# Linear attention and an MLP in one kernel: another hand-set order of the same operations, with the first group's loads ahead of the second slice of w_in

## The chip, the cores and the metric

The kernel runs on one core of a Trainium2 chip. The metric is the device time of one execution in microseconds; each kernel's time is the median of several executions.

A core has five engines that run side by side, each through its own queue in order: PE (matrix products), DVE (vector work), ACT (activation functions, also copies), POOL (vector work, and here the issuing of all loads that convert from 32-bit to 16-bit floats), and SP (the issuing of the stores, of the transposes done by the DMA engines, and of one small load). An instruction waits for the data or the buffer that it needs, and everything behind it on its engine waits with it.

## The reference: what is computed

A causal attention with a decay per head, in blocks of 64 positions with a running state, and behind it an MLP with an exact GELU on all 3072 tokens (4 batches of 768):

```python
for b in range(nb):                       # 12 blocks of 64 positions
    intra = einsum('bhic,bhjc->bhij', qb, kb) * Dmask       # Dmask = lam ** (i - j), lower triangle
    intra = einsum('bhij,bhjd->bhid', intra, vb)
    inter = einsum('bhid,bhde->bhie', qb * lam_pow, kv_state)
    out[:, :, sl] = intra + inter
    kv_state = lam_block * kv_state + einsum('bhsd,bhse->bhde', kb * rev_pow, vb)
x = out.transpose(0, 2, 1, 3).reshape(3072, 512)
h = x @ w_in                              # 512 -> 2048
g = 0.5 * h * (1 + erf(h / sqrt(2)))
return g @ w_out                          # 2048 -> 512
```

## The kernel before

**Tiling.** The sequence is cut into six groups of 128 positions (g = 0 to 5). A group has 4 batches, taken as two pairs (p = 0, 1), so 512 tokens. Per group the kernel does the attention of both pairs, then the first product (x by w_in) with the GELU, and then the second product (by w_out) with the stores. Weights stay in SBUF. Accumulators are eight PSUM banks: M0, M1, M2 for the first product, N0, N1 mostly for transposes and the second product, X0, X1 for attention scores and outputs, KV for the state.

**The order is written out.** Each step is registered with a name, an engine, what it reads and what it writes. `emit` then issues the steps in the sequence of the text ORDER, so that ORDER sets the queue of each engine; the tile framework adds the waits that reads and writes need. Steps with a choice of engine (`"ACT|DVE"` and the like) go to the first one unless the name in ORDER has a suffix such as `/DVE`. The prices given with the steps serve a planner outside the kernel and have no effect when it runs.

**Names.** Digits are group and pair, then a part.

- `ld.q00a`, `ld.k00b`, `ld.v01a`: loads of q, k, v for group 0; a and b are the two batches of a pair (128 KB each, L323). `ld.q10` and so on: loads of a whole pair for later groups (256 KB, L316). `ld.wi0`, `ld.wi4`, `ld.wi8`, `ld.wi12`: four slices of w_in (512 KB, L336). `ld.wo00` to `ld.wo11`: four quarters of w_out (512 KB, L341). All are issued by POOL.
- `trow`, `tpos`, `tdl`, `tex`, `tmk`, `tid`, `cols`: small tables on DVE and PE (L200 to L239); `ln`, `etab`, `xv2`, `xg0`, `xg1`, `xx`, `xq`, `xv`, `xc`: powers of lambda on ACT (decay L243, lam_x L234); `tg0`, `tg1`: their masks on DVE; `gtab` (L279) loads the GELU table on ACT after the last of these.
- `idle0`, `idle1`, ...: dummy matmuls of 128x512 on zeros (L879), as many as IDLES says; `bits` is one more.
- `Tq00a`, `Tk00a`: transposes of q and k on PE for groups 0 and 1 (L550, L405); `Eq000`, `Ek000`: their copies out of PSUM (L304 on ACT, L306 on DVE). From group 2 the transposes are DMAs issued by SP (L416).
- Group 0: `sc000`, `sc001` scores; `m0000` and so on masks times decay (L611, DVE); `vh000` v scaled by the decay (L528); `o000`, `o001` outputs; `x000`, `x001` copies into x; `ka00a`, `ka00b` states and `sa00a` their decay. Later groups: `u` scores and first half of the state, `m`, `sm` (a copy of the state), `i` the contribution of the state and the second half, `o`, `x` (L517), `ks` and `sa`; `vh` scaled v (L366 ACT, L369 DVE or POOL).
- `H0.3.0`: first product of group 0, two columns of 128 (number 3 of 8) for pair 0, 8 matmuls of 128x256; `g0.3.0` its GELU (L673). `H0.0.x` and `H0.1.x` read ld.wi0, `H0.2.x` and `H0.3.x` ld.wi4, 4 and 5 ld.wi8, 6 and 7 ld.wi12. `h1.1.5`: one of seven products that replace eight (Strassen-Winograd) in later parts, with sums `V`, `X`, `W`, `S` and `hm`, `hs`, `ha`, `hb`, `g` around them. `Q0.0a` to `Q3.0d`: second product of group 0; `Q0.0b` reads ld.wo10. `P` with `pm`, `ps`, `pa`, `c11`, `c12`, `c21`, `c22`: second product of later groups; `st`, `sp`: stores.

**Buffers around the change.** Raw q, k and v have four buffers each, used in turn by group and pair; scaled v (`vh`) has two, so that `vh21` must wait until `o11` has read `vh11`. The sequence of the steps in which they are registered (L946 on) decides which of two steps on the same buffer comes first.

All matrix products are recorded with line L283, all copies with L304 or L306.

Of the kernel before, what the change touches and what calls it, by code (L numbers as in the profile page):

```python
# [30 lines left out]
sa11 V0.2 H0.4.1 g0.6.0 g0.6.1 H0.7.1 vh201/ACT o11 Tk21 H1.0.0 x111 vh211/POOL g0.4.1 g0.7.1 x110 H0.7.0 g1.0.0 X0.1
ld.wo00 Tq20 V2.1 h1.1.5 V0.0 H1.5.0 X1.1 hm1.1 X2.1 ks20 hs1.1/DVE H1.1.0 V0.3 Tk20 h1.1.6 g1.1.0 h1.1.2 g0.7.0
H1.0.1 g1.1.00 g1.5.0 H1.4.0 ha1.1 g1.0.1 Tq21 X3.1 H1.4.1 g1.4.0 V1.2 V3.2 h1.1.7 vh200 g1.4.1 H1.1.1 hb1.1 ld.v40
h1.3.5 V2.3 g1.1.1 W0.0 h1.1.3 ld.wo10 h1.1.4 V1.0 u20 g1.1.10 ld.wo01 H1.5.1 g1.1.01 m201 ld.wo11 sm20 m200 Q0.0a
g1.5.1 ld.v30 i20 ld.k30 h1.3.1 sa20 Q1.0a hs1.3 V1.3 ld.q30 V3.3 hm1.3 h1.3.6 g1.1.11 o20 ha1.3 ks21 ld.k31 h1.3.2
x201 vh210/ACT h1.3.3 x200 Q0.0b ld.v31 V3.0 u21 S0.1.2 S2.1.0 h1.3.7 sm21 V2.0 m211 Q1.0b g1.3.00 m210 Q0.0c hb1.3
Q1.0c S0.1.4 i21 Q0.0d sa21 S1.1.2 h1.3.4 W1.0 q0.0 Q1.0d ks30 g1.3.10 Q2.0a q1.0/DVE S0.1.0 o21 h2.0.1 x210 Q2.0b
hs2.0 x211 g1.3.01 Q3.0a X0.2 Tq30 g1.3.11 S3.1.2 X1.2 h2.0.5 S1.1.4 h2.0.6 X2.2 hm2.0 Tk30 vh300 Q2.0c ha2.0 Q3.0b
S0.1.6 h2.0.2 h2.0.7 Tk31 g2.0.00 vh311/POOL h2.0.3 hb2.0 h2.1.1 g2.0.01 X3.2 Q3.0c vh301/POOL vh310 h2.0.4 h2.1.5
g2.0.10 ld.q31 u30 hm2.1/DVE hs2.1 Q3.0d m300 sm30 ld.q40 m301 h2.1.6 q3.0 h2.1.2 ha2.1 g2.0.11 i30 g2.1.00 W0.1  # L40
h2.1.7 sa30/ACT S2.1.4 h2.1.3 hb2.1 h2.2.1 S0.2.0 g2.1.01 Q2.0d V2.2 ks31 Tq31 h2.1.4 g2.1.11 q2.0/DVE h2.2.5 g2.1.10
S2.1.2 o30 W1.1 hm2.2 sp0.1 P5.1a vh400/POOL sp0.0 hs2.2/DVE Tq40 P5.1b x301 vh401/POOL x300 h2.2.6 h2.2.2 ha2.2
ld.k40 u31 g2.2.00 sp0.2 h2.2.7 m310 sm31 P1.1a pm.1 ld.v41 hb2.2 m311 h2.3.1 h2.2.4 S1.1.0 S3.1.4 i31 g2.2.10 h2.2.3
hs2.3/DVE P1.1b g2.2.01 sa31 S0.2.2 h2.3.6 ps.1/DVE h2.3.5 S1.1.6 h2.3.2 Tk40 hm2.3 S2.1.6 o31 ks40 S3.1.0 P2.1a ha2.3
g2.2.11 sp0.3 x310 g2.3.00 h2.3.7 vh410/POOL h2.3.3 hb2.3 P2.1b S2.2.0 ld.v51 g2.3.11 x311 h2.3.4 c11.1 h3.0.1 W2.0
# [4 lines left out]
ld.q51 h3.2.1 S1.2.6 h3.1.4 S2.2.4 sm41/DVE P5.2a g3.1.10 c12.1/DVE g3.1.11 h3.2.5 m410 hs3.2 P5.2b hm3.2 S1.2.2 m411  # L50
h3.2.6 P1.2a S2.3.2 S3.2.4 S3.2.2 h3.2.2 ha3.2 i41 S3.2.0 Tq50 S0.3.0 h3.2.7 sa41 h3.2.3 hb3.2 P1.2b Tk50 g3.2.01
S1.3.0 g3.2.00 S3.2.6 h3.2.4 pm.2 S2.2.6 h3.3.5 ps.2 h3.3.1 o41 g3.2.10 st1.00 P2.2a vh510/POOL vh511 hs3.3 st1.11
ks50 st1.01 x411 h3.3.6 g3.2.11 P6.2a S2.2.2 hm3.3 x410 h3.3.2 ha3.3 P2.2b h3.3.7 h3.3.3 hb3.3 u50 g3.3.01 S0.3.4
# [72 lines left out]
def kernel(  # L126
# [207 lines left out]
    def add_w_in(kf0, kf1):  # L334
        f = slice(kf0 * 128, kf1 * 128)
        add("ld.wi%d" % kf0, "POOL", lambda: nc.gpsimd.dma_start(w_in[:, :, f], w_in_r[:, :, f]), (),  # L336
            ["wi%d.%d" % (kf, kh) for kf in range(kf0, kf1) for kh in range(2)], ("w", kf1 - kf0))
# [667 lines left out]
```

## Time and profile before

| | before |
|---|---|
| median of 3 runs | 207.84 us (206.88 to 209.09) |
| profiled execution, its own time | 207.61 us |
| its span, first to last instruction | 205.8 us |
| PE busy | 194.6 us (95%) |
| DVE busy | 145.6 us (71%) |
| ACT busy | 104.8 us (51%) |
| POOL busy | 62.2 us (30%) |
| dummy matmuls, without `bits` | 32 |

The profile is of one execution. Times are from the first instruction of the span. A row of records in order of time gives the start, the duration from the first start to the last end of the merged instructions, engine, line, operation, what it writes and reads, sizes and how many; in brackets stands how long the engine had been idle just before, and what ended that. Rows of groups give busy time in all and the mean of one in ns. Durations of matmuls contain the way through the array, so that the next may start before one ends; 16 matmuls of 128x256 end to end take about 1.75 us at full clock. "PEclk" is the clock that PE was granted, as a share of full speed. For loads the profile gives the time from the issue on POOL to the landing; KB are those of the 16-bit destination.

### The profile page before, as it was taken

To read this page: it belongs to the slowest core of one execution; us is meant where nothing else is said; L and a number is where in the kernel's file an instruction comes from. 1 tells how busy PE (TensorE), PEld (TensorE's weight loads), DVE (VectorE), ACT (ScalarE), POOL (GpSimd) and SP (SyncE) were. 2 spreads that over 40 slices of the span, in tenths; PEclk is the share of its full clock that TensorE was granted. 3 is DMA by queue.
4 is the path that set the end of the run, shared out by engine and by line. 5 is a ranking of instruction groups with operands and counts; after the bars stand their busy time and mean duration, and the time that the engine had idled before them with its cause. 6 is when DMAs were issued, how large, how long until landed. Compare 5 with 4: busy or idle time off the path is not lost. (4 is left out here: it accounts for less than half of the span.)

```text
span 205.8 us, 6791 instructions
## 1 busy us (share of the span) xinstructions
PE 194.6 (95%) x2955; PEld 155.4 (76%) x2955; DVE 145.6 (71%) x317; ACT 104.8 (51%) x211; POOL 62.2 (30%) x73
## 2 busy tenths in 40 slices
...
PEclk9999699999999999999999999999999999999999
...
GB/s 61 179 172 188 180 164 177 157 146 153 113 180 189 157 179 85 209 136 178 69 138 103 123 113 230 5 178 80 54 0 105 0 5 0 22 185 1 155 51 154
DMA packets 95598, 24.56 MB, mean 119 GB/s; under 512 B 85840, under 2 KB 95056, under 8 KB 95568
## 3 DMA queue, kind: packets, MB, share of 16 engines
...
q14 instruction: 7, 0.06, 0.1%
...
## 5 line engine op out<-in xcount | busy, mean ns | idle before, releaser
L765 ACT ACTIVATE g<-M 128x512 bf16<-128x512 f32 x51 | 29.9, 598 | 47.8 <-PE M L283 47.1
L283 PEld LDWEIGHTS <-w_in 128*128 128x128 bf16 x480 | 46.1, 99 | 9.0 <-issue 0.8
L283 PE MATMUL M<-x,w_in 128*128 128x256 bf16 x328 | 45.2, 279 | 1.3 <-DMA w_in<-in_moe_w_in_dram 0.7
L283 PEld LDWEIGHTS <-g 128*128 128x128 bf16 x304 | 29.2, 98 | 10.2 <-issue 2.1
L283 PE MATMUL N<-w_out,g 128*128 128x256 bf16 (+1 forms) x224 | 35.9, 303 | 0.8 <-DMA w_out<-in_moe_w_out_dram 0.8
L283 PEld LDWEIGHTS <-S 128*128 128x128 bf16 x320 | 30.9, 98 | 3.7
L369 POOL TENSOR_TENSOR vh<-vr,lam_v 128x256 bf16<-128x256 bf16 x18 | 12.0, 688 | 53.4 <-DMA vr<-in_v_dram 27.8
L283 PEld LDWEIGHTS <-V 128*128 128x128 bf16 x216 | 20.9, 98 | 4.2 <-issue 0.9
L283 PE MATMUL M<-xs,w_in 128*128 128x256 bf16 x136 | 20.5, 273 | 0.0
L283 PE MATMUL M<-xs,V 128*128 128x256 bf16 x136 | 19.4, 273 | 0.0
L673 ACT ACTIVATE g<-M 128x512 bf16<-128x512 f32 x24 | 13.3, 601 | 10.2 <-PE M L283 9.9
L283 PE MATMUL N<-T,S 128*128 128x256 bf16 x144 | 18.2, 273 | 0.0
L691 DVE TENSOR_TENSOR S<-g 128x512 bf16<-128x512 bf16 x40 | 16.4, 417 | 2.0 <-ACT g L765 2.0
L784 DVE TENSOR_TENSOR m<-m,M 128x512 f32<-128x512 f32 x17 | 11.7, 686 | 8.6 <-PE M L283 5.4
L283 PE MATMUL N<-w_out,S 128*128 128x256 bf16 x144 | 17.5, 273 | 0.0
L517 DVE TENSOR_TENSOR x<-X,lam_x 128x512 bf16<-128x512 f32 x20 | 13.2, 683 | 5.1 <-PE X L283 5.0
L283 PE MATMUL KV<-vh,kr 64*64 64x64 bf16 x352 | 15.9, 196 | 0.6 <-DVE vh L528 0.4
L485 DVE TENSOR_TENSOR scm<-X,mask 128x512 bf16<-128x512 f32 x20 | 13.3, 686 | 3.8 <-PE KV L283 3.8
L283 PEld LDWEIGHTS <-kr 64*64 64x64 bf16 x352 | 13.9, 108 | 1.1 <-issue 1.0
L316 POOL DMA_DIRECT2D vr<-in_v_dram x10 | 11.8, 1176 | 8.8 <-ACT g L673 7.1
L779 DVE TENSOR_TENSOR M<-m,M 128x512 f32<-128x512 f32 x17 | 11.7, 690 | 2.8 <-ACT g L765 1.7
L765 ACT ACTIVATE g<-m 128x512 bf16<-128x512 f32 x18 | 11.4, 634 | 1.6 <-DVE m L784 1.6
...
## 6 DMA issues: line engine op xcount, KB each, us to landing
out_dram<-osb SPq DMA_DIRECT2D x22, 256.0 KB, 2.5
vr<-in_v_dram POOLq DMA_DIRECT2D x10, 256.0 KB, 9.2
kr<-in_k_dram POOLq DMA_DIRECT2D x10, 256.0 KB, 9.5
qr<-in_q_dram POOLq DMA_DIRECT2D x10, 256.0 KB, 8.3
w_in<-in_moe_w_in_dram POOLq DMA_DIRECT2D x4, 512.0 KB, 8.0
w_out<-in_moe_w_out_dram POOLq DMA_DIRECT2D x4, 512.0 KB, 8.5
qr<-in_q_dram POOLq DMA_DIRECT2D x4, 128.0 KB, 5.7
kr<-in_k_dram POOLq DMA_DIRECT2D x4, 128.0 KB, 5.8
```

What stands on the lines that cost most here:

```text
L283: nc.tensor.matmul(*a, skip_group_check=True, **kw)
L316: add("ld.%s%d%d%s" % (n, g, p, suffix(cs)), "POOL", lambda: nc.gpsimd.dma_start(dst, source(n, g, p, cs)), (), rkeys(n, g, p, cs), ("load ...
L369: ENG[e].tensor_mul(o_[:, c, h0:h1], v_[:, c, h0:h1], lam_v[:, h0:h1, None].to_broadcast((128, h1 - h0, D)))
L485: add(name("m", hi), "DVE", lambda hi=hi: nc.vector.tensor_mul(m_[:, hi, cr], sc[hi][:, cr], mask[:, None, None, :].to_broadcast((128, nc_ ...
L517: add(name("x", bl), "DVE", lambda bl=bl: nc.vector.tensor_mul(x_[:, cr, :, half(bl)], o[bl][:, cr], lam_x[:, None, :, half(bl)].to_broadc ...
L673: lambda: nc.scalar.activation(gt[g % 2][:, 2 * j:2 * j + 2, t], seen(bk, "n t", n=2), ACT.Gelu),
L691: lambda i=i, op=op, l=l, r=r: nc.vector.tensor_tensor(s(i)[0], l[0], r[0], op), l[1] + r[1], s(i)[1],
L765: lambda: nc.scalar.activation(gt[g % 2][:, 4 * c + fo:4 * c + 3 + fo:2, th * 2 * C:(th + 1) * 2 * C], src, ACT.Gelu),
L779: add("ha" + nm, "DVE", lambda: nc.vector.tensor_add(seen(bc, "q t", q=2), f5, seen(bb, "q t", q=2)), [bb, k5], [bc], ("ps", 512))
L784: add("hb" + nm, "DVE", lambda: nc.vector.tensor_add(f7, f5, seen(bb, "q t", q=2)), [bb, k5], [k7], ("ps", 512))
```

## The change

ORDER is another sequence of the same operations, from its first line to the first product of group 3; behind that the two are alike. There are six groups of dummy matmuls instead of eight (26 matmuls instead of 32). For 31 steps the engine is another: 16 copies, products and scalings leave DVE (11 for ACT, 5 for POOL), 12 come to DVE from ACT, one goes from ACT to POOL, and two from POOL to ACT.

The loads of group 0 (twelve) now all stand ahead of ld.wi0, and ld.v10, which stood among them, stands behind ld.wi0, ld.q10, ld.k10 and three scalings that POOL does (vh000, vh011, vh010; before, POOL did vh000 and vh101 there). The tables xx and xq stand ahead of the first copies on ACT. ld.wo10, ld.wo01 and ld.wo11 stand right behind ld.wo00; before, ld.v40 stood between.

The three other edits do not change what is issued: the condition on neg2 and lam_q2 was false before too (PAIRED holds no 1), WSPLIT gives the slices that the loop gave, and 600 is a price for the planner.

```diff
-IDLES = (4, 13, 1, 1, 1, 3, 8, 1)
+WSPLIT = ((0, 4), (4, 4), (8, 4), (12, 4))
+IDLES = (3, 12, 1, 8, 1, 1)
 
 ORDER = """
-tb0 ldlam trow ld.wi4 ld.q00b ld.k00a idle0 tpos ln bits tdl etab ld.q00a tmk ld.k00b tid tex ld.v00a cols xv2 ld.v00b
-xg1 ld.k01b xg0 ld.q01b tg1 idle1 Tq00b ld.k01a Eq001/DVE idle2 Tk00a ld.q01a tg0 Ek000 idle3 Tq00a ld.v10 xv
-Eq000/DVE idle4 Tk00b Ek001 ld.v01b xc idle5 sc000 ld.v01a sc001 m0000 vh000/POOL m0001 m0010 vh001 ld.wi0 idle6 Tk01a
-o000 m0011 ld.k10 ka00a sa00a idle7 o001 ka00b x000 ld.q10 Tk01b x001 Ek011/DVE Tq01a Ek010/DVE xq xx Tq01b sa00b
-vh101/POOL H0.3.0 Eq011/DVE Eq010 vh010 ld.wi8 gtab sc011 vh011 sc010 ld.q11 V0.1 ka01a m0100 ld.k11 m0111 H0.1.0
-m0101 ld.v11 H0.0.0 sa01a m0110 o010 ld.wi12 g0.0.0 o011 Tk10 g0.1.0 ld.v21 x011 ka01b Ek101/DVE x010 vh100 Tq10
-ld.k20 sa01b H0.0.1 Eq100 Eq101/DVE Ek100 ks10/DVE H0.1.1 ld.v20 g0.0.1 g0.3.0 u10 ld.k21 H0.4.0 m100 m101 H0.2.1
+tb0 ldlam trow bits ld.wi4 ld.k00b ld.q00a idle0 tpos ln tdl etab ld.q00b tex ld.k00a cols tmk xv2 ld.q01b xg0 tid
+ld.v00a ld.v00b xg1 tg0 ld.q01a V0.1 xx ld.v01b tg1 idle1 Tq00a ld.k01b xq xv xc Eq000 Tq00b ld.v01a Tk00b Eq001/DVE
+Ek001 Tk00a ld.k01a Ek000/DVE gtab ld.wi0 idle2 sc000 sc001 m0000 ld.q10 m0011 m0001 ld.k10 m0010 idle3 o000 vh001
+vh000/POOL idle4 o001 x001 Tk01b x000 idle5 Tq01b vh011/POOL ka00a Ek011 Eq011/DVE Tq01a sa00a Tk01a Eq010 Ek010/DVE
+ka00b vh010/POOL H0.3.0 sa00b sc010 ld.v10 sc011 m0101 ka01a H0.0.0 m0111 ld.q11 m0100 H0.1.0 g0.0.0 m0110 ld.wi8 o010
+sa01a o011 ld.k11 Tq10 x010 ka01b g0.1.0 sa01b Tk10 x011 Ek101/DVE H0.0.1 ks10/DVE Ek100/DVE H0.1.1 vh100/ACT
+vh101/POOL Eq100/DVE Eq101/DVE V1.1 g0.1.1 ld.v11 u10 Tq11 m101 sm10 ld.wi12 H0.2.0 g0.0.1 m100 ld.k21 H0.2.1 g0.2.0
...
-        if 1 in PAIRED:
+        if 1 in PAIRED and 1 in QSG:
...
-                over(["x%d%d%d" % (g % 2, p, i) for i in range(2)], (ch,)), ("acp", 512))
+                over(["x%d%d%d" % (g % 2, p, i) for i in range(2)], (ch,)), ("acp", 600))
...
-    for s in range(0, NKF, 4):
-        add_w_in(s, s + 4)
+    for s, n in WSPLIT:
+        add_w_in(s, s + n)
```

The rest of group 0 and the loads behind it, as far as the prediction speaks of them (new order):

```
i10 ld.v20 g0.2.1 H0.3.1 sa10 ld.q21 Eq110/DVE H0.5.0 g0.3.1 g0.3.0 ld.k20 Tk11 Eq111 H0.4.0 g0.5.0 vh110/POOL vh111
o10 g0.4.0 H0.4.1 x100 Ek110 ks11 ld.q20 x101 H0.5.1 Ek111 ld.v21 u11 g0.5.1 V0.3 h1.1.1 m110 sm11 H0.6.1 g0.4.1 m111
...
V1.0 H1.5.1 V2.3 g1.1.1 X2.1 Tk21 V3.0 h1.1.2 g1.5.1 V0.2 h1.1.6 g1.1.00 vh211/POOL h1.3.1 H1.4.1 hs1.3/DVE ld.wo00
ha1.1 h1.3.6 g1.4.1 X3.1 ks20 ld.wo10 h1.1.7 hb1.1 u20 ld.wo01 m200 sm20 h1.1.4 ld.wo11 h1.3.5 V3.1 g1.1.10 m201
```

More of the change, by code (lines that the diff above doesn't have):

```diff
@@ L31 @@
[L31 to L45, printed above, removed]
@@ new lines @@
+i10 ld.v20 g0.2.1 H0.3.1 sa10 ld.q21 Eq110/DVE H0.5.0 g0.3.1 g0.3.0 ld.k20 Tk11 Eq111 H0.4.0 g0.5.0 vh110/POOL vh111
+o10 g0.4.0 H0.4.1 x100 Ek110 ks11 ld.q20 x101 H0.5.1 Ek111 ld.v21 u11 g0.5.1 V0.3 h1.1.1 m110 sm11 H0.6.1 g0.4.1 m111
+i11 H0.6.0 H0.7.0 g0.6.0 g0.6.1 H0.7.1 o11 Tq21 g0.7.1 H1.0.0 x111 g0.7.0 x110 H1.1.0 g1.0.0 vh201 Tk20 H1.4.0 g1.1.0
+X0.1 V1.3 X1.1 h1.1.5 g1.4.0 H1.5.0 hm1.1/DVE sa11/ACT V3.3 Tq20 H1.0.1 vh200 hs1.1 V0.0 H1.1.1 g1.0.1 V2.1 g1.5.0
+V1.0 H1.5.1 V2.3 g1.1.1 X2.1 Tk21 V3.0 h1.1.2 g1.5.1 V0.2 h1.1.6 g1.1.00 vh211/POOL h1.3.1 H1.4.1 hs1.3/DVE ld.wo00
@@ new lines @@
+ha1.1 h1.3.6 g1.4.1 X3.1 ks20 ld.wo10 h1.1.7 hb1.1 u20 ld.wo01 m200 sm20 h1.1.4 ld.wo11 h1.3.5 V3.1 g1.1.10 m201
+h1.3.2 ld.q30 hm1.3 g1.1.11 i20 ha1.3 vh210/POOL h1.1.3 sa20 h1.3.7 g1.1.01 ks21/DVE h1.3.3 ld.k30 g1.3.00 hb1.3 Q0.0a
+g1.3.01 S2.1.0 ld.v30 h1.3.4 V1.2 S0.1.2 o20 W0.0 Q1.0a ld.q40 S2.1.2 V2.0 Q0.0b x201 x200 Q1.0b S0.1.0 u21 h2.0.1
+m210 sm21 Q1.0c g1.3.11 V3.2 m211 g1.3.10 Q0.0c hs2.0/DVE i21 W1.0 h2.0.2 S1.1.2 W0.1 Q0.0d V2.2 S2.1.6 Q1.0d q0.0
+sa21 Q2.0a q1.0 ks30 o21 g2.0.00 Q2.0b x211 Tk30 x210 Q3.0a X2.2 Tq30 X0.2 Q3.0b vh300/POOL X1.2 h2.0.5 S0.1.6 h2.0.6
@@ new lines @@
+ld.q31 hm2.0 S0.1.4 h2.1.1 vh301/ACT ha2.0 Q2.0c ld.k31 X3.2 h2.0.7 h2.0.3 hb2.0 ld.v31 Q3.0c g2.0.01 g2.0.11 h2.0.4
+h2.1.5 g2.0.10 u30 hs2.1 Q2.0d m301 sm30 m300 hm2.1 Q3.0d Tq31 W2.0 h2.1.6 S1.1.4 q3.0 i30 ha2.1 Tk31 h2.1.2 sa30
+P5.1a g2.1.00 S1.1.0 S1.1.6 ks31 h2.1.7 S3.1.2 h2.2.1 hb2.1 vh310/POOL o30 sp0.3 h2.1.3 Tq40 x300 h2.1.4 g2.1.01 x301
+vh311/POOL P5.1b g2.1.10 q2.0 h2.2.5 ld.k40 hs2.2 u31 hm2.2/DVE g2.1.11 h2.2.2 m310 sm31 ld.v40 h2.2.6 m311 g2.2.00
+P1.1a ha2.2 i31 S0.2.2 S3.1.0 h2.2.7 h2.2.3 hb2.2 h2.3.1 g2.2.01 S3.1.4 h2.2.4 pm.1 W1.1 o31 g2.2.10 Tk40 P1.1b
```

20 lines of the change are left out of this document (10 added, 10 removed).

## The prediction

> **What bounds the kernel now.** I read the page first, then the busy times by stage, the PE records of the first 30 us in order of time, and last the loads. The page:
>
> ```profile
> PE 194.6 (95%) x2955; PEld 155.4 (76%) x2955; DVE 145.6 (71%) x317; ACT 104.8 (51%) x211; POOL 62.2 (30%) x73
> PEclk9999699999999999999999999999999999999999
> ```
>
> PE is busy 95% of the 205.8 us span, and one slice in 40, around 20 to 26 us, ran at a lower clock. The stages (columns: length, then busy time of PE, PEld, DVE, ACT and POOL, then granted clock, DMA share, GB/s):
>
> ```profile
> 17.30:28.70 11.40, 9.68 (x155) 7.19 (x152) 7.34 (x15) 6.85 (x14) 9.32 (x10) 0.85 1.96 178
> 28.70:61.00 32.30, 31.73 (x609) 25.99 (x609) 20.34 (x43) 21.57 (x47) 13.56 (x16) 1.00 1.67 154
> 61.00:62.00 1.00, 0.17 (x2) 0.10 (x1) 1.00 (x3) 0.64 (x3) 1.00 (x2) 1.00 1.21 194
> 62.00:112.80 50.80, 50.80 (x844) 38.34 (x843) 41.81 (x84) 27.81 (x57) 18.79 (x23) 1.00 1.49 145
> 113.60:184.90 71.30, 71.26 (x948) 62.22 (x948) 54.92 (x113) 34.20 (x63) 4.11 (x5) 1.00 0.50 79
> ```
>
> From 28.7 us on PE is nearly gapless: it loses 0.57, 0.83, 0.00 and 0.04 us in the four later rows, and what these rows leave out is short (about 0.5 us between 112.8 and 113.6, 0.85 at 184.9, and the last stores). So an earlier arrival of PE at its dense work should come out at the end almost whole, as long as DVE (41.81 of 50.80 us from 62 to 112.8), ACT and the loads keep up. What can be saved lies ahead of 28.7 us, and in the one gap at 61. PE there, in order of time:
>
> ```profile
> 3.35 3.45 PE L879 MATMUL M<-idle 128*128 128x512 bf16 x13
> 7.75 0.44 PE L550 MATMUL N<-ident,qr 64*64 64x64 bf16 x16 [0.95 <-DMA qr<-in_q_dram]
> 11.25 0.42 PE L283 MATMUL X<-qT,kT 64*64 64x128 bf16 x16
> 11.82 1.90 PE L879 MATMUL M<-idle 128*128 128x512 bf16 x8
> 17.27 1.05 PE L283 MATMUL M<-x,w_in 128*128 128x256 bf16 x8
> 18.68 0.42 PE L283 MATMUL N<-qT,kT 64*64 64x128 bf16 x16 [0.37 <-ACT qT L304]
> 21.11 3.37 PE L283 MATMUL M<-x,w_in 128*128 128x256 bf16 x16 [0.71 <-DMA w_in<-in_moe_w_in_dram]
> 24.41 0.81 PE L283 MATMUL X<-scm,vr 64*64 64x128 bf16 x32
> 26.88 1.91 PE L283 MATMUL M<-x,w_in 128*128 128x256 bf16 x16 [0.19 <-ACT x L304]
> 28.71 0.22 PE L283 MATMUL X<-qT,kT 64*64 64x64 bf16 x4
> 61.87 1.02 PE L283 MATMUL N<-w_out,g 128*128 128x512 bf16 x4 [0.83 <-DMA w_out<-in_moe_w_out_dram]
> ```
>
> The 17.27 row is H0.3.0, the first dense product; 21.11 is H0.1.0 and H0.0.0, which waited for the second w_in slice (ld.wi0) and then took 3.37 us where the same 16 matmuls at 26.88 (H0.0.1, H0.1.1) took 1.91; 28.71 is u10, where group 1 begins. 61.87 is Q0.0b, waiting for ld.wo10.
>
> **The loads.** Issues on POOL in order (start, duration), and four answers on time from issue to landing: the first ld.wi4, ld.wi0, ld.v10, and ld.v40 issued at 53.09 with nothing queued ahead.
>
> ```profile
> 1.27 0.94 POOL L336 DMA_DIRECT2D w_in<-in_moe_w_in_dram  x1 [0.82 <-POOLq L989]
> 7.28 0.68 POOL L323 DMA_DIRECT2D qr<-in_q_dram  x1 [0.23 <-DMA w_in<-in_moe_w_in_dram]
> 8.98 0.68 POOL L323 DMA_DIRECT2D qr<-in_q_dram  x1 [0.31 <-DMA kr<-in_k_dram]
> 9.65 1.16 POOL L316 DMA_DIRECT2D vr<-in_v_dram  x1
> 12.24 1.08 POOL L528 TENSOR_TENSOR vh<-vr,lam_v 128x512 bf16<-128x512 bf16 x1
> 13.22 0.83 POOL L336 DMA_DIRECT2D w_in<-in_moe_w_in_dram  x1
> 53.09 1.15 POOL L316 DMA_DIRECT2D vr<-in_v_dram  x1 [7.12 <-ACT g L673]
> ```
>
> ```profile
> w_in<-in_moe_w_in_dram POOLq DMA_DIRECT2D x1, 512.0 KB, 5.7
> w_in<-in_moe_w_in_dram POOLq DMA_DIRECT2D x1, 512.0 KB, 7.8
> vr<-in_v_dram POOLq DMA_DIRECT2D x1, 256.0 KB, 7.9
> vr<-in_v_dram POOLq DMA_DIRECT2D x1, 256.0 KB, 5.8
> qr<-in_q_dram POOLq DMA_DIRECT2D x4, 128.0 KB, 5.7
> ```
>
> So wi4 landed at 1.27 + 5.7 = 7.0 and wi0 at 13.22 + 7.8 = 21.0. Between them landed twelve loads of 128 KB, v10 of 256 KB and wi0 of 512 KB: 2304 KB in 14.0 us, 164 KB per us. Loads therefore queue, and a load lands when the bytes ahead of it are through (not under 5.5 to 5.8 us after issue): 0.78 us for 128 KB, 1.56 for 256, 3.1 for 512. The ninth issue (7.28) waited for the first landing and the eleventh (8.98) for the third: eight are in flight at most, and I keep that rule.
>
> **The change, part by part.** The condition on neg2 was false before as well, the slices of WSPLIT are the old four, and the 600 is only a planner's price: these three cost nothing. IDLES drops 6 of 32 dummy matmuls, all of which lie in waits.
>
> *Loads.* All twelve of group 0 go first; ld.wi0 moves from sixteenth to fourteenth, ld.v10 from twelfth to seventeenth, behind three POOL multiplies (vh000, vh011, vh010). Landings by the rate: k00b 7.7, q00a 8.7, k00a (fifth, as k00b was before) 10.1, k01b 14.7, v01a 15.5, k01a 16.3; wi0 at 16.3 + 3.1 = 19.4, or 18.9 with its old 7.8 us from an issue at 11.05: I take 19.0, 2 us sooner. Then q10, k10 and v10 at 1.56 each: 20.6, 22.4 and 24.1 (before, v10 landed at 9.65 + 7.9 = 17.6). POOL is not what holds v10: two multiplies from v01a on, 15.5 + 2 x 1.08 = 17.7, plus the 5.8 us of an empty queue is 23.5.
>
> *PE up to H0.3.0.* DVE and ACT rows that the walk uses (a pair of mask products takes 1.29, so one every 0.6):
>
> ```profile
> 11.70 1.29 DVE L611 TENSOR_TENSOR scm<-X,decay 128x512 bf16<-128x512 f32 x2 [1.36 <-PE X L283]
> 8.23 0.42 DVE L306 COPY qT<-N 128x512 bf16<-128x512 bf16 x1 [0.84 <-PE N L550]
> 5.32 2.86 ACT L243 ACTIVATE decay<-delta,ln 128x192 bf16<-128x192 f32 x8
> 15.52 1.32 ACT L304 CAST x<-X 128x512 bf16<-128x512 f32 x2 [4.22 <-PE X L283]
> 16.89 1.27 ACT L234 ACTIVATE lam_x<-rowx,ln_col 128x128 f32<-128x128 f32 x4
> L673 ACT ACTIVATE g<-M 128x512 bf16<-128x512 f32 x24 | 13.3, 601 | 10.2 <-PE M L283 9.9
> L366 ACT ACTIVATE vh<-vr,lam_v 128x128 bf16<-128x128 bf16 x4 | 1.3, 396 | 0.0
> ```
>
> The tables now run through on ACT: decay until 8.2, lam_x (xx, moved up from 16.89) until 9.4, the three small ones until 9.9. Eq000 and Ek001 queue behind them, and end by 10.9. That costs nothing, because Tk00a waits for k00a at 10.1 and its copy (0.42, now on DVE) ends at 11.0; were the tables over 0.1 us longer, the excess would be on the path. sc000 starts at 11.1 (11.25 before). Four masks at 0.6 and vh001 follow on DVE; o000 starts after idle3 (8 dummies, 1.9 us) at 13.6, o001 at 14.1, and x001, x000 (1.32) end at 15.9, where they ended at 16.84. They no longer set the end: k01a does, at 16.3. Tk01a, ka00b, then H0.3.0 at 17.0, 0.27 sooner.
>
> *From H0.3.0 to u10.* H0.3.0 takes 0.9 (17.9). qT and kT are copied by then, as lam_x and the gelu table (gtab) no longer stand ahead of Eq010 on ACT, so sc010, sc011 and ka01a follow at once (18.9; 20.4 before). H0.0.0 and H0.1.0 start with wi0 at 19.0 and take 1.75 at full clock, to 20.8; o010, o011 0.8, Tq10 0.55, ka01b 0.3, Tk10 0.55: 23.0. H0.0.1 waits for x010 and x011 on ACT, which have g0.1.0 (0.6) between them: 21.6 + 0.66 + 0.6 + 0.66 = 23.5. The 16 matmuls end at 25.3. u10 needs v10 at 24.1 and then vh100 (1.3 on ACT) or vh101 (1.2 on POOL): 25.5 instead of 28.71. **Minus 3.2 us.** This stage has two clocks of nearly the same length, PE at 25.3 and v10 at 25.5.
>
> *After u10.* By the rate k11 lands at 30.4, v11 at 31.9, wi12 at 35.0, all ahead of their first users (Tk11 at 30.9, u11 at 34.4, H0.6.1 at 35.7); the last slack is 0.7 us. These times count PE's products on from u10 at 0.9 each. Two waits are new in their place: vh101 on POOL waits for v10 with v11, wi12 and group 2's loads behind it, and V0.3 on DVE waits for wi12 (35.0) with u11's masks (35.5 at the earliest) behind it; both fit. vh211 on POOL waits for v21, now the last of group 2's loads (35.0 + 6 x 1.56 = 44.4), and ends at 45.6; w_out's four loads follow it without v40 between: wo00 5.8 to 6.5 us later, wo10 3.1 after that, 55. Q0.0b comes at about 58 (61 less 3.2). **Minus 0.83 us.** Only SP's order of transposes changes otherwise (Tq21 first); they end some 3 us ahead of u20. Sixteen copies and products leave DVE and twelve come to it, so it is lighter by some 2.6 us (four of 0.6 to 0.7), and POOL, idle 70%, takes four more. New gaps in the reordered part I bound by what the old order shows there, 0 to 1.1 us (0.57 and 0.5), and take as much as before: nothing either way. From h3.3.6, in the first product of group 3, the order is the old one.
>
> *The clock.* Three stretches (same columns):
>
> ```profile
> 7.70:11.11 3.41, 3.12 (x70) 1.81 (x70) 1.31 (x3) 1.77 (x6) 3.06 (x5) 1.00 1.80 177
> 17.95:21.36 3.41, 1.88 (x55) 1.31 (x53) 2.68 (x5) 2.17 (x4) 3.41 (x5) 1.00 1.90 178
> 21.36:24.77 3.41, 3.41 (x32) 2.27 (x33) 1.73 (x4) 0.25 (x1) 2.50 (x3) 0.50 1.84 186
> ```
>
> After 3.41 us with 1.88 us of PE work the clock was halved for as long again; that cost 3.37 - 1.91 = 1.5 us. The new order keeps 18 to 25 us full, but opens another hole: dummies end at about 6.4, the next work is Tq00a at 8.7, and up to 11.1 there are four transposes of 0.44 and one dummy, some 1.9 us of 4.7. I expect one halved stretch there. It slows sc000 and the dummies of idle3, not loads; H0.3.0 comes 0.3 to 0.9 later, of which the wait for wi0 and v10 swallows some. **Plus 0.5** (0 to 1.2).
>
> The Trainium skill, "TensorE: Matmul & The Clock Gate", section "HAM oscillation — how this bites in real kernels", gives as the abstract rule that no idle gap should exceed about 3.4 us. By it neither 21.36 (longest gap 0.71) nor the new hole (2.3) would halve the clock; the trace disagrees at 21.36, and the measurement decides.
>
> **Sum.** The profiled execution took 207.61 (span 205.8 and 1.8 around it). 207.61 - 3.2 - 0.83 + 0.5 = 204.1; the median of the three runs is 0.23 above the profiled one, so 204.3.
>
> **Rivals.**
> - *The clock does not fall in the new hole.* What speaks for it: 2.5 us of work in 4.28 to 7.70 was enough before, and that stretch still holds 2.1. Against: 1.88 was not enough. It gives 203.8. It is what the rule of the Trainium skill named above would give too.
> - *v10 decides.* If its 256 KB wait for one load more (1.56), u10 stands on PE with everything behind it: 205.9. For: 24.1 is worked out from a mean rate, and PE is level with it. Against: the bytes ahead of it are fewer than in any other order with wi0 first.
> - *The new order's waits eat it.* DVE or ACT stalls PE between 30 and 110 us for what the opening won: each late step costs about 0.6, and five such give 207.3. Against: lighter DVE, no gap from 62 to 112.8 today.
> - *Slower: half clock on dense work.* If the thin stretch is followed by others (17 to 25 us with wi0 or v10 later than I have them), each halved stretch of full PE work costs 1.7 us (3.41 / 2). Two give 207.7, three 209.4, and from the third on it is slower than before. Against: 3.1 us of work in each stretch by my walk.
>
> **How the numbers follow.** Forecast 0.42, no fall of the clock 0.22, v10 0.14, new waits 0.12, half clock 0.10 (0.04 with three stretches or more). A measurement here tells 1% from no change: 205.8 and 209.9. The first two lie below 205.8, and so does a third of the v10 case and of the waits: 0.72. Slower is the three stretches and 0.02 for a chain I don't see: 0.06. Within 1%: 0.22. The range reaches from the case in which the old gaps of 1.1 go too without a fall of the clock (203.8 - 1.1 = 202.7) to the v10 case with its clock term at the upper end (205.9 + 0.7 = 206.6).
>
> **What would show it.** H0.3.0 at about 17.0, H0.0.0 without a wait over 0.5 us for w_in, sc010 right behind H0.3.0; u10 at about 25.5 with v10 landing near 24.1; no wait for w_out ahead of Q0.0b; clock at 0.5 somewhere between 8.5 and 14.5 us and at 1.00 from 18 on. I am wrong if u10 comes later than 27, if the halved stretch lies on dense products, or if PE shows gaps of over 1 us together between 30 and 110.

## The result and the profile after

The new order is slower by half a per cent, not faster: 208.44 us median (20 executions, 207.37 to 212.75) against 207.68 (20 executions) for the kernel before on the same chip. The ratio is 1.0053, 95% interval 1.0033 to 1.0074. The forecast was 204.3. Medians here and below are over all executions; ratios leave out the executions that took over 1.5% longer than the fastest of their kernel, as some executions of most kernels do.

| | before | after |
|---|---|---|
| profiled execution, its own time | 207.61 us | 207.91 us |
| its span | 205.8 us | 206.1 us |
| PE busy | 194.6 us | 194.3 us |
| H0.0.0 (or H0.1.0) starts | 21.11 us | 20.18 us |
| u10 starts | 28.71 us | 27.68 us |
| last group's P4.4a starts | 185.75 us | 185.66 us |

The page of the kernel after: PE's busy time, the granted clock in 40 slices, and the DMA queue q8, which the page calls "instruction" (transfers, MB, share).

```profile
PE 194.3 (94%) x2949; PEld 154.9 (75%) x2949; DVE 147.7 (72%) x310; ACT 105.2 (51%) x211; POOL 68.1 (33%) x79
...
PEclk9969999999999999999999999999999999999998
...
q8 instruction: 23, 0.38, 0.8%
```

The first four of the stages shown for the kernel before (length, then busy time of PE, PEld, DVE, ACT and POOL, clock, DMA share, GB/s), and then the stretch ahead of the clock's fall and the halved one:

```profile
17.30:28.70 11.40, 9.99 (x255) 8.17 (x255) 7.31 (x17) 5.32 (x12) 8.29 (x10) 1.00 2.12 170
28.70:61.00 32.30, 30.48 (x545) 25.23 (x545) 23.09 (x43) 20.92 (x41) 18.39 (x20) 1.00 1.75 174
61.00:62.00 1.00, 1.00 (x36) 0.60 (x32) 1.00 (x3) 0.00 (x0) 0.00 (x0) 1.00 2.30 160
62.00:112.80 50.80, 50.76 (x838) 37.76 (x837) 41.35 (x80) 28.84 (x61) 22.13 (x24) 1.00 1.53 134
```

```profile
6.70:10.11 3.41, 1.97 (x52) 1.10 (x50) 1.65 (x4) 3.41 (x13) 2.82 (x5) 1.00 1.77 173
10.11:13.52 3.41, 3.36 (x54) 1.87 (x53) 2.17 (x5) 2.15 (x4) 3.29 (x5) 0.50 1.81 178
```

The clock fell where it was expected, and the gap at 61 is gone. But from 28.7 to 61 PE now idles 1.82 us, where it idled 0.57. PE's records in order of time (start, duration, operation; in brackets the idle time before and what ended it):

```profile
11.33 0.64 PE L284 MATMUL X<-qT,kT 64*64 64x128 bf16 x16
12.33 2.47 PE L880 MATMUL M<-idle 128*128 128x512 bf16 x8
18.38 1.05 PE L284 MATMUL M<-x,w_in 128*128 128x256 bf16 x8
19.36 0.42 PE L284 MATMUL X<-qT,kT 64*64 64x128 bf16 x16
20.18 1.92 PE L284 MATMUL M<-x,w_in 128*128 128x256 bf16 x16
22.03 0.69 PE L284 MATMUL X<-scm,vr 64*64 64x128 bf16 x26
23.67 0.30 PE L284 MATMUL X<-scm,vr 64*64 64x128 bf16 x6 [0.95 <-issue]
25.85 1.91 PE L284 MATMUL M<-x,w_in 128*128 128x256 bf16 x16 [0.40 <-ACT x L305]
27.68 0.22 PE L284 MATMUL X<-qT,kT 64*64 64x64 bf16 x4
43.09 0.38 PE L284 MATMUL M<-x,w_in 128*128 128x256 bf16 x2 [0.69 <-issue]
47.12 0.60 PE L284 MATMUL N<-xs,V 128*128 128x256 bf16 x4 [0.56 <-DVE xs L718]
53.81 0.60 PE L284 MATMUL M<-xs,V 128*128 128x256 bf16 x4 [0.41 <-DVE M L307]
185.66 1.03 PE L284 MATMUL N<-T,g 128*128 128x256 bf16 x8 [1.18 <-DVE osb L842]
```

The two rows with "issue" are new: PE stops in the middle of o011 (after 26 of the 32 matmuls of o010 and o011, for 0.95 us) and in the middle of H0.7.1 (0.69 us), with every operand there, and the profile shows nothing that it waited for. The profile of the kernel before has no such row. Counted from the first matmul, the two gaps stand behind record 351 and record 735 (a record is one matmul of the profile). Their distance is 384 = 3 x 128 matmuls, each with its weight load: 3 x 256 instructions. A place where a new block of 256 would begin is called a boundary below; record 351 stands at the third, record 735 at the sixth. The queue q8 brings 23 transfers for 5,898 matmuls and weight loads, one per 256. So the theory that the experiments tested: *PE reads its instructions in blocks of 256, and in the opening, where the loads fill the DMA engines, the next block is not there in time when PE goes through its small matmuls too fast.* Its rivals: the gaps belong to o011 and H0.7.1 themselves; the clock decides; or the loss comes from the rest of the new order.

### The profile page after: what moved, and what is told of

The parts are those of the page before. It is cut to its first block, busy times and chain, and to the rows that moved or that the text cites. A ratio compares the mean times of both kernels' runs of the same rounds, so it can differ in the third digit from the quotient of the medians.

```text
span 206.1 us, 6771 instructions
## 1 busy us (share of the span) xinstructions
PE 194.3 (94%) x2949; PEld 154.9 (75%) x2949; DVE 147.7 (72%) x310; ACT 105.2 (51%) x211; POOL 68.1 (33%) x79
## 5 line engine op out<-in xcount | busy, mean ns | idle before, releaser
L284 PEld LDWEIGHTS <-w_in 128*128 128x128 bf16 x480 | 45.5, 98 | 8.7 <-issue 1.9
L284 PE MATMUL M<-x,w_in 128*128 128x256 bf16 x328 | 43.4, 273 | 1.1 <-issue 0.7
L284 PE MATMUL N<-w_out,g 128*128 128x256 bf16 (+1 forms) x224 | 35.4, 303 | 0.0
L370 POOL TENSOR_TENSOR vh<-vr,lam_v 128x256 bf16<-128x256 bf16 x22 | 15.6, 728 | 55.1 <-DMA vr<-in_v_dram 43.8
L317 POOL DMA_DIRECT2D kr<-in_k_dram x10 | 11.9, 1188 | 0.0
L317 POOL DMA_DIRECT2D qr<-in_q_dram x10 | 11.8, 1186 | 0.0
```

The source lines that it names most:

```text
L284: nc.tensor.matmul(*a, skip_group_check=True, **kw)
L317: add("ld.%s%d%d%s" % (n, g, p, suffix(cs)), "POOL", lambda: nc.gpsimd.dma_start(dst, source(n, g, p, cs)), (), rkeys(n, g, p, cs), ("load ...
L370: ENG[e].tensor_mul(o_[:, c, h0:h1], v_[:, c, h0:h1], lam_v[:, h0:h1, None].to_broadcast((128, h1 - h0, D)))
```

## The experiments

Ratios are to the kernel before on the same chip, with 95% intervals.

**Which half of the order (e2, e3).** e2 is the new ORDER up to o10 with the remaining steps in the old sequence, e3 the reverse; the sources are otherwise those of after and before.

> The new order up to o10, then what is left in the order of before. In the two profiles the new order stood 1.03 us ahead at u10 and at i11. If the later part of the new order gave that back by its waits on DVE and ACT: about 1 us faster than before (206.7). If the lead is lost in any case (a fetch of instructions or a load is what paces both until 43 us): the same as before within 0.4 us, with a gap without releaser in o011 (0.9 us) as in the new order, and with the wait for w_out at Q0.0b (0.8 us) as in before.

> The order of before up to o10, then what is left in the new order. If the later part of the new order is what costs: slower than before by 1.0 to 1.5 us (208.7 to 209.2). If the later part is as good as the old one: 207.2 to 207.7, that is up to 0.5 us faster, as the wait for w_out (0.83) goes. The gap in o011 should not be there, as PE enters that block later.

e2: 210.29 us, 1.019 (1.0143 to 1.0237). e3: 217.22 us, 1.0527 (1.0466 to 1.0588). Both are worse than either parent, outside all that was expected, so they split nothing. New waits come with the joint: in e2 PE waits 1.40 us at 38.13 for a copy of the state on ACT, in e3 u20 waits for one of SP's transposes (the second of the two rows shown for e7 and e3 below). e2 has the gap in o011 as well (0.72, ended at 23.70).

**The clock (e1, e5, e8).** e1 adds eight dummy matmuls to the new order's hole, e5 five to the old order's, e8 takes eight away from the new order:

```diff
 # e1, new order
-IDLES = (3, 12, 1, 8, 1, 1)
+IDLES = (3, 18, 1, 2, 8, 1, 1)      # one between Tq00a and Tq00b, two ahead of sc000
 # e8, new order
+IDLES = (3, 11, 1, 1, 1, 1)
 # e5, old order: dummies behind H0.3.0 (1), sc010 (1), ka01a (3)
+    for i, n in enumerate((1, 1, 3)):
+        add_idle("warm%d" % i, n, "M0")
```

> The new order with eight dummy matmuls more (18 instead of 12 behind tpos, one between Tq00a and Tq00b, two instead of one ahead of sc000), so that PE has work in the hole between 7.5 and 11.3 us. Clock theory (the halved stretch at 10.1 to 13.5 us made H0.3.0 late, 18.4 instead of the forecast 17.0): no clock of 0.5 ahead of H0.3.0, H0.3.0 at about 17.3, u10 at about 26.7 instead of 27.7, time 0.5 to 1.0 us under that of the new order (207.4 to 207.9). Instruction theory (PE's instructions come in blocks of 256 by DMA, one block ahead, and a block takes about 6.1 us while the loads run): two gaps with no releaser stay, at the 16 instructions earlier places, and eat part of it. If the clock was not what cost time: u10 stays at 27.7.

> The order of before with five dummy matmuls (128x512, bank M0) more in the waits between H0.3.0 and H0.1.0 (one ahead of sc011, one ahead of ka01a, three behind ka01a). Clock theory: the stretch of 3.41 us around 18 to 21.4 us then holds about 3 us of work, the clock stays at 1.00 there, H0.1.0 and H0.0.0 take 1.9 instead of 3.4 us: 1.0 to 1.5 us faster than before in the executions that have the halved stretch. As instructions move by 10 places, the third block of PE's instructions is reached about 1 us sooner; if its fetch is not in by then, a gap without releaser stands at matmul 351 and the gain is under 0.5 us. If the clock did not matter: no change.

> The new order with eight dummy matmuls fewer (idle1 11 instead of 12, idle3 1 instead of 8), so that the third boundary, at matmul 351 of the record, falls on the third transpose of Tq10 instead of the tenth product of o011. Instruction theory: a gap without releaser stands there, it ends at 23.5 to 23.8 us as in the four runs so far, and u10 comes at 27.2 to 27.8 although o000 and H0.3.0 come up to 0.8 us sooner than in the new order. If the instructions were not what PE waits for: no such gap, u10 at about 26.5.

e1: 207.95 us, 1.0069 (1.0035 to 1.0103). The clock stayed full until 23.6, H0.3.0 came at 17.36 as expected, and o010 came 1.03 us sooner than in the new order (21.00 against 22.03); all of it was lost again. PE's records of e1:

```profile
17.36 1.05 PE L284 MATMUL M<-x,w_in 128*128 128x256 bf16 x8
21.00 0.58 PE L284 MATMUL X<-scm,vr 64*64 64x128 bf16 x18
23.74 0.63 PE L284 MATMUL X<-scm,vr 64*64 64x128 bf16 x14 [2.15 <-issue]
28.70 0.22 PE L284 MATMUL X<-qT,kT 64*64 64x64 bf16 x4
```

Eight matmuls more stand ahead, and PE stops eight matmuls sooner in o010 and o011 (after 18 of the 32 instead of 26): again behind record 351. It goes on at 23.74, where the new order went on at 23.67. The wait then halved the clock (23.6 to 27.0), and u10 starts at 28.70, as before the change. e5: 206.97 us, 0.9987 (0.9951 to 1.0023), clock at 1.00 throughout, u10 at 27.28 instead of 28.71, and a gap marked "issue" of 0.37 in H0.7.1; the 1.4 us gained at u10 against the one profile of the kernel before don't come out in the times (see "The old order's halved stretch" below). e8: 208.82 us, 1.0052 (1.0013 to 1.0091): the gap expected in Tq10 did not come. The clock is halved from 11.3 to 21.6, and PE reached record 351 only at 24.02, later than it went on behind the gap in the new order. The clock alone doesn't decide; dummies that fill the holes bring the boundary sooner.

**The w_out loads (e6, e7).** The old order with ld.v40 behind ld.wo11, alone (e6) and with e5's dummies (e7):

```diff
-... ld.wo00 ... ld.v40 ... ld.wo10 ... ld.wo01 ... ld.wo11 ...
+... ld.wo00 ... ld.wo10 ... ld.wo01 ... ld.wo11 ld.v40 ...
```

> The order of before with one step moved: ld.v40 behind ld.wo11 instead of behind ld.wo00. The part of the change that the prediction priced at 0.83 us, alone. If the wait for w_out ahead of Q0.0b is all that ld.v40 causes: that wait is gone and the time 0.5 to 0.8 us under before (ratio 0.996 to 0.998). If something else is late next (DVE's sums of w_out, the stores, v40 itself): no change.

> The order of before with both: the five dummies and ld.v40 behind w_out. If the two costs are separate: 1.5 to 2.2 us faster than before (ratio 0.989 to 0.993). If PE's instructions or the loads pace the stretch up to 43 us anyway: no more than the 0.5 to 0.8 us of ld.v40.

e6: executions from 207.1 to 217.9 us, ratio 1.0045 (0.9994 to 1.0096). e7: 1.0115 (1.0043 to 1.0186). The wait for w_out goes, and another takes its place in e7 and e3 (u20, waiting for SP's transposes of q and k):

```profile
57.15 0.22 PE L283 MATMUL X<-qT,kT 64*64 64x64 bf16 x4 [2.28 <-DMA kT<-kr]
```

```profile
60.28 0.27 PE L283 MATMUL X<-qT,kT 64*64 64x64 bf16 x4 [2.55 <-DMA qT<-qr]
```

SP issues the four transposes in another sequence in the old order than in the new one. In e7 the second of the two that u20 needs is issued at 45.52, 0.1 us ahead of w_out's first load (45.63), and lands at 57.10. In the kernel after it is issued at 45.27, 1.5 us ahead of w_out's first load (46.74), lands at 49.57, and u20 has no such wait.

**Instructions ahead of the gap (e4).** The new order with 40 small matmuls (64x64 on zeros, 80 instructions) behind idle1, in a hole:

```diff
+            for i in range(n):      # n = 40
+                mm(bank[bk][half(i % 2), :D], idle[half(i % 2), :D], idle[half(i % 2), :D], start=True, stop=True)
```

> The new order with 40 small dummy matmuls (64x64 by 64x64, 80 instructions) behind idle1, in the hole in which PE waits for q00a, so that every later instruction stands 80 places further on in the program. Instruction theory: blocks begin at instructions 256 n - 66 of the records, so the third boundary moves from matmul 351 (in o011) to the third matmul of H0.0.0; a gap without releaser of about 2.5 us stands there, between the crossing of the second boundary (in Tq01b, about 16.8) and 6.1 us after it (22.9), and none in o011. Time 0.5 to 1.4 us over the new order. Rival (the gap belongs to o011: a wait that the profile doesn't show, on DVE or on a bank): the gap of about 1 us stays in o011, at the same matmul, and the time stays within 0.4 us of the new order.

210.23 us, 1.0174 (1.0112 to 1.0235). The gap left o011 for H0.0.0:

```profile
20.41 0.39 PE L284 MATMUL M<-x,w_in 128*128 128x256 bf16 x2
23.51 1.69 PE L284 MATMUL M<-x,w_in 128*128 128x256 bf16 x14 [2.70 <-issue]
25.13 0.64 PE L284 MATMUL X<-scm,vr 64*64 64x128 bf16 x32
```

It stands behind record 351 once more, two matmuls into a step that had no gap in the new order, and it ends at 23.51. The place moves with the count, the end does not: that refutes the rival that o011 or its operands cause it.

**All gaps of the kind.** The 19 profiles have 24 gaps of PE of over 0.3 us marked "issue", all between 16 and 94 us. Counted in weight loads, they stand multiples of 128 apart (those behind 90 us one short of that). Each ends 1.29 to 1.81 us after a transfer on q8 has ended, so what ends it is, as far as the profiles show, a block that has come. The old order is not free of them: e3 and e7 stop behind record 223 (0.52 and 0.72 us), e5, e6 and e7 behind record 735 (0.37, 1.32 and 0.99). e7:

```profile
16.73 0.22 PE L550 MATMUL N<-ident,kr 64*64 64x64 bf16 x2 [0.72 <-issue]
```

**Fewer instructions (f1 to f4).** The eight transposes of group 0 take 128 columns each instead of 64, so 64 matmuls (128 instructions) are gone ahead of the gap. The kernels leave out the right order of the transposed halves, so that their output is not the reference's:

```diff
-                    for hi in range(2):
-                        nc.tensor.transpose(b16[ch][half(hi), hp, par], src[half(ch), hp, hi, par], ident[half(ch), half(ch)])
+                    nc.tensor.transpose(b16[ch][:, hp, par], src[half(ch), hp, par].rearrange("p s d -> p (s d)"), ident[half(ch), half(ch)])
```

> The new order, but each of the eight TensorE transposes of the first group takes 128 columns at once: 8 matmuls instead of 16, 64 matmuls (128 instructions) fewer before the boundary at which the new order stopped. It leaves out the right order of the transposed halves (head and token parity change places), so the output is not the reference's; every shape and byte count stays. Theory (a block of 256 TensorE instructions that is not there before about 23.7): the third boundary now falls 64 matmuls later, in H0.1.1, which is reached after 24 anyway, so the gap of 0.95 in o011 goes; the sixth moves to about 47, so the gap of 0.69 goes too; u10 at 25.5 to 26.8 (27.68 in the new order), the time 1 to 2 below the new order's, 0.99 to 0.998 of before. Rival (the gap in o011 belongs to the new order's place of o011, not to the count of instructions): gap of about 1 again in o011, time as the new order, 1.005.

> The same halved transposes (same part left wrong) in the new order with the eight warming matmuls of e1. Theory: clock full throughout the first 23; the third boundary is reached at 22 to 23 in H0.0.1 or H0.1.1 and passed at about 23.7, a gap of 0.5 to 1.5 instead of 2.39; u10 at 25.5 to 27 (28.70 in e1); the time 1.5 to 2.5 below e1's ratio of 1.0069, so 0.994 to 1.000. Rival (gap tied to o011): gap of 2.4 in o011 again, ratio 1.007.

> The old order with the same halved transposes (same part left wrong). It has no gap at the third boundary to lose; its opening waits for loads. Theory: u10 within 0.7 of 28.71, time 0.995 to 1.002 of before. Rival (halved transposes are a gain of their own, whatever the order): as much gain here as in the new order, 0.99 or below.

> The old order with five warming matmuls (e5) and the halved transposes (same part left wrong). Theory: the gap of 0.64 at the sixth boundary goes, since that boundary moves from 41.4 to about 45; u10 as in e5; time 0.3 to 0.7 below e5's, ratio 0.994 to 0.998. Rival: 0.999 as e5.

f1: 204.08 us, 0.9855 (0.981 to 0.9899). f2: 204.27, 0.9864 (0.9824 to 0.9905). f3: 205.65, 0.9933 (0.99 to 0.9967). f4: 206.36, 0.9965 (0.9934 to 0.9995). The new order gains 2.0% of it (1.0053 to 0.9855), the old one 0.7%. f1 in order of time, then f3:

```profile
18.31 1.05 PE L284 MATMUL M<-x,w_in 128*128 128x256 bf16 x8
21.95 0.76 PE L284 MATMUL X<-scm,vr 64*64 64x128 bf16 x32
24.61 1.91 PE L284 MATMUL M<-x,w_in 128*128 128x256 bf16 x16 [0.43 <-ACT x L305]
26.45 0.22 PE L284 MATMUL X<-qT,kT 64*64 64x64 bf16 x4
```

```profile
21.16 1.92 PE L283 MATMUL M<-x,w_in 128*128 128x256 bf16 x16 [0.50 <-DMA w_in<-in_moe_w_in_dram]
27.52 0.22 PE L283 MATMUL X<-qT,kT 64*64 64x64 bf16 x4
```

H0.3.0 in f1 is where it was (18.31 against 18.38), with the clock halved at nearly the same time (10.3 to 13.7), and o010 starts at 21.95 against 22.03, so the shorter transposes themselves gain nothing up to there. o010 and o011 now run through, 32 matmuls in 0.76 us, and u10 starts 1.23 us sooner than in the new order. The third boundary, expected in H0.1.1, lies behind the first products of u10: PE passes it at 26.5, 2.9 us after the transfer from 22.64 to 23.64 has ended. At the second gap's place it is 2.0 ahead (o11 at 41.4 against 43.4). f2's opening was held by a load (0.92 ahead of Tk01a) and not by the boundary, against its expectation, and its time is f1's.

More came at the end: the gap of 1.18 ahead of P4.4a is gone in f1 and in f3. That was not expected; f1, f2 and f3 gained more than expected (f4 as much). g1 and g2 test the cause.

**The end of the program (g1, g2).** DVE's c22.4 waits until an earlier store has read its buffer. Four stores leave SP together there, because three that could go (group 3's) stand behind st4.00. PE's row with the wait in the kernel before, then DVE in the kernel after, and the DMA engines over 6 us from the first store's start, in 40 slices, after and then f1:

```profile
185.75 1.03 PE L283 MATMUL N<-T,g 128*128 128x256 bf16 x8 [0.89 <-DVE osb L841]
```

```profile
184.92 0.69 DVE L842 TENSOR_TENSOR osb<-m5o,N 128x512 f32<-128x512 f32 x1 [1.76 <-DMA out_dram<-osb]
```

```profile
GB/s 218 355 294 362 375 314 300 375 369 335 314 314 369 355 348 314 348 335 341 328 321 7 0 0 0 0 7 7 7 14 14 20 27 14 0 0 0 0 0 0
...
q8 instruction: 1, 0.02, 1.0%
```

```profile
GB/s 198 341 300 355 375 321 287 389 362 341 335 287 375 355 355 335 328 362 348 335 273 34 0 0 0 0 0 0 0 0 0 0 0 0 0 0 0 0 0 0
```

The four stores (1,088 packets) take 3.21 us in f1 and f3 and 3.22 in f4, in which no instruction transfer falls among them. In after one does (182.40 to 183.33), and 17 packets wait for its end: 5.06 us until the last. Before, e1 and e5 are alike (4.86, 4.57 and 4.91, each with a transfer among them). g1 and g2 put the three stores right behind the copies that fill them:

```diff
-... c22.3 ... c12.3 ... c21.3/DVE ... st4.00 ... st3.10 ... st3.01 ... st3.11 ...
+... c22.3 st3.11 ... c12.3 st3.01 ... c21.3/DVE st3.10 ... st4.00 ...
```

> The new order with three output stores (st3.11, st3.01, st3.10) each right behind the copy that fills its buffer, instead of behind st4.00 in SP's queue. Theory (an instruction fetch that falls among four stores issued together makes the last land 1.4 to 1.9 later, and c22.4 waits for that store): the wait for the store and TensorE's gap of 1.18 ahead of P4.4a go, the time falls 0.9 to 1.3 below the new order's, 0.998 to 1.002 of before. Rival (the gap comes from VectorE or TensorE, the store is only the last event): the gap stays, 1.005.

> The old order with the same three stores moved. Theory: the gap of 0.89 ahead of P4.4a goes, 0.994 to 0.997 of before. Rival: 1.000. If both g1 and g2 gain the same, the end of the program has no part in the new order's loss.

g1: 207.35 us, 1.0002 (0.9963 to 1.0041). g2: 206.32 us, 0.9925 (0.988 to 0.997). The wait of DVE and PE's gap are gone in both, and both gain about what was expected (0.5% and 0.75%, of which 1.18 and 0.89 us are 0.57% and 0.43%). So the end is a fault of both orders, and no cause of the difference between them. g1's profile shows what the gap in o011 can do besides:

```profile
23.96 0.30 PE L283 MATMUL X<-scm,vr 64*64 64x128 bf16 x6 [1.63 <-issue]
26.14 3.43 PE L283 MATMUL M<-x,w_in 128*128 128x256 bf16 x16 [0.40 <-ACT x L304]
29.49 0.22 PE L283 MATMUL X<-qT,kT 64*64 64x64 bf16 x4
```

The clock had stayed full in that execution; the wait of 1.63 halved it, on dense products (3.43 instead of 1.91), and u10 came 0.8 later than before the change.

**With everything computed (g3, g4, g5).** Group 0's q and k are loaded with the two token parities apart, so that a transpose of 128 columns gives the right layout. g3 does it for the second pair, g4 for both, g5 for both in the old order; all three have the moved stores.

```diff
+        if p in SWAP and n != "v":
+            dst = raw[n][buf(g, p, NR[n])][half(ch)].rearrange("p (s h d) -> p s h d", s=2, h=H)
+            src = dram[n][2 * p + ch, :, g * C:(g + 1) * C, :].rearrange("h (i s) d -> i s h d", s=2)
```

> As g1, and q and k of the second pair of the first group are loaded with the two token parities apart, so that their four transposes take 128 columns each: 32 matmuls (64 instructions) fewer ahead of the third boundary, all computed. The price: these four loads move pieces half as long. Theory: the boundary falls ahead of H0.0.1, reached after 24, so no gap of 0.95 in o011; u10 1 earlier than in the new order if the loads cost nothing, 0 if they cost 0.25 us each; 0.988 to 0.998 of before. Rival (the loads' price is the larger): H0.0.0 1 later, time as g1.

> As g3 for both pairs: 64 matmuls fewer, as in f1, but all computed. Theory: no gap at the third nor at the sixth boundary, as f1 (0.9855) plus what eight loads in shorter pieces cost, 0 to 2: 0.985 to 0.996. Rival (the loads' price is the larger): sc000 and H0.3.0 1 to 2 later, 0.998 to 1.005.

> The old order with the stores moved (as g2) and the shorter transposes of both pairs (as g4), everything computed. Theory (the new order's opening is the better one once the instructions are there in time; the old order's opening waits for loads and gains nothing from fewer instructions): no better than g2's 0.9925, and by the loads' price worse, 0.993 to 0.999, so above g4's 0.990. Rival (halved transposes and moved stores explain g4 whatever the order): 0.988 or below.

g3: 206.89 us, 0.9987 (0.995 to 1.0024), not to be told from g1. With 32 matmuls fewer the boundary falls into Tk10, and the gap moved there instead of going (below): the expectation had the place nearly right and the end wrong.

```profile
24.04 0.28 PE L409 MATMUL N<-ident,kr 128*128 128x128 bf16 x2
25.04 0.49 PE L409 MATMUL N<-ident,kr 128*128 128x128 bf16 x6 [0.72 <-issue]
```

g4: **204.92 us, 0.9900 (0.9849 to 0.9951)**, the fastest of the kernels that compute everything, ahead of both orders as given. From g2 (0.9925), the old order with the stores moved, its interval does not separate it. It has no gap of the kind before 60 us. It pays for its loads: sc000 starts at 11.89, the clock is halved twice as long (9.5 to 16.4), and u10 starts at 28.16. g5: 207.33 us, 0.9987 (0.9957 to 1.0017): in the old order the price of the loads eats the gain, and PE waits for them:

```profile
21.65 0.31 PE L283 MATMUL KV<-vh,kr 64*64 64x64 bf16 x8 [1.03 <-DVE vh L531]
29.00 0.22 PE L283 MATMUL X<-qT,kT 64*64 64x64 bf16 x4
```

All together (ratio to before):

| | old order | new order |
|---|---|---|
| as given | 1 | 1.0053 |
| stores moved (g2, g1) | 0.9925 | 1.0002 |
| transposes halved, their right order left out (f3, f1) | 0.9933 | 0.9855 |
| stores moved, shorter transposes, all computed (g5, g4) | 0.9987 | 0.9900 |

The new order loses 0.5 to 0.8% with the full count of instructions, and is ahead by 0.8 to 0.9% with 64 matmuls fewer in group 0 (g4 and g5 ran on two chips, each against the kernel before on its own).

## Why the prediction was wrong

**The step that failed is "From H0.3.0 to u10", minus 3.2 us.** It was to bring u10 to 25.5 and brought it to 27.68, minus 1.03. Of the 2.2 us missing, 1.23 are the stop in o011, by f1, and about 1 comes from the late H0.3.0 (next paragraph). The sequence held, but it left out that PE needs its instructions: the walk had o011 done by 21.6, and PE did not pass record 351 before 23.5 in any variant of the new order with full transposes and a gap there (after 23.67, e1 23.74, e2 23.70, e4 23.51, g1 23.96; in g3, where this is a later matmul, 25.04). With the transposes halved that is no longer in the way, and u10 starts at 26.45, 2.26 sooner than in the profile of the kernel before.

**The clock's fall, plus 0.5.** Right in its place (10.11 to 13.52, on scores and dummies; 1.97 us of PE work in the 3.41 us ahead of it) and in the full clock from 13.5 on. Its price was too low: the two scores took 0.64 each instead of 0.42 and idle3 2.47 instead of 1.9, and H0.3.0 came at 18.38, 1.4 later than walked, where 0.3 to 0.9 was allowed. f1 shows what was left of it at u10: 26.45 against 25.5, so about 1.

**The old order's halved stretch** was counted as a property of the kernel (3.37 against 1.91 us at H0.1.0 and H0.0.0, 1.5 of the 3.2). It belongs to the profiled execution and not to every one: g2 has the opening of the kernel before, and its profiled execution kept the clock at 1.00 (H0.1.0 and H0.0.0, then u10):

```profile
20.97 1.92 PE L282 MATMUL M<-x,w_in 128*128 128x256 bf16 x16 [0.37 <-DMA w_in<-in_moe_w_in_dram]
27.14 0.22 PE L282 MATMUL X<-qT,kT 64*64 64x64 bf16 x4
```

Against that u10 of the new order (27.68) is later, and f1's (26.45) only 0.7 sooner. Between f1 and f3, both with halved transposes, it is 1.07.

**The loads.** The rate of 164 KB per us held up to k10 (landed 22.6, forecast 22.4); v10 came 0.9 later than by the rate. wi0 and v10 in the kernel after (issue on POOL, then the time to landing, then the scaling that waits for v10):

```profile
11.14 0.76 POOL L337 DMA_DIRECT2D w_in<-in_moe_w_in_dram  x1
17.76 1.21 POOL L317 DMA_DIRECT2D vr<-in_v_dram  x1
25.15 1.18 POOL L370 TENSOR_TENSOR vh<-vr,lam_v 128x256 bf16<-128x256 bf16 x2 [3.12 <-DMA vr<-in_v_dram]
```

```profile
w_in<-in_moe_w_in_dram POOLq DMA_DIRECT2D x1, 512.0 KB, 7.8
```

```profile
vr<-in_v_dram POOLq DMA_DIRECT2D x1, 256.0 KB, 7.2
```

wi0 landed at 11.14 + 7.8 = 18.9 (forecast 19.0), and H0.0.0 had no wait for it. v10 landed at 17.76 + 7.2 = 25.0 (forecast 24.1). It did not decide, but it stands right behind the gap: vh101 ends at 26.3, and f1's u10 starts at 26.45.

**After u10.** The wait for w_out went as forecast (61.00 to 62.00: 1.00 busy), and no wait for SP's transposes took its place, as one did in e7. "Nothing either way" for new gaps was wrong: 0.69 in H0.7.1, 0.56 and 0.41 behind it, and 1.18 instead of 0.89 at P4.4a. At P4.4a PE is 0.09 ahead of before, and its last product starts 0.09 sooner too (200.69 against 200.78); the 0.3 us by which the span is longer lie in the stores behind it.

**The rivals.** The nearest is "the new order's waits eat it" (207.3, given 0.12), with another mechanism: not DVE or ACT, but instructions. "v10 decides" and "half clock on dense work" did not happen in the profiled execution; the second did in e1 and g1, behind the gap. The case of three halved stretches, 209.4, was counted as slower, though it lies below the bound of 209.9 that the prediction itself sets.

The Trainium skill, "Runtime: NRT & Kernel Launch", section "Instruction fetch mechanics", says that instructions come in blocks of 256 and that the cost of a block boundary is mostly hidden. The block size agrees with the count above; that it is hidden doesn't hold here, with gaps of 0.69 us in the kernel after to 2.70 us in e4.
